# New durations, margins and preferences in the plan of an attention and two-layer MoE kernel, with some low halves on other engines

## The chip, the cores and the metric

The kernel runs on one core of one Trainium2 chip. The metric is the device time of one launch in microseconds (us); several launches are timed and their median is given. One more launch was recorded by the hardware profiler, and all rows below are from that one. The engines are PE (TensorE), ACT (ScalarE), DVE (VectorE), POOL (GpSimd) and SP (SyncE, which here only starts DMA transfers); each works through its own instructions in order.

## The reference

```python
# q, k, v: (4, 8, 576, 64) float32
scores = (1.0 / np.sqrt(64)) * np.matmul(q, k.transpose(0, 1, 3, 2))
kth = np.partition(scores, -32, axis=-1)[..., -32:-31]
scores = np.where(scores >= kth, scores, -1000000000.0)
attn = np.exp(scores - np.max(scores, axis=-1, keepdims=True))
attn = attn / (np.sum(attn, axis=-1, keepdims=True) + 1e-09)
x = np.matmul(attn, v).transpose(0, 2, 1, 3).reshape(2304, 512)
h = x @ moe_w_in                 # 512 x 2048
x = np.maximum(0.01 * h, h) @ moe_w_out   # 2048 x 512
h = x @ moe2_w_in
out = (h * (1.0 / (1.0 + np.exp(-h)))) @ moe2_w_out
```

Each row of 576 scores keeps its 32 largest. The 2304 tokens then go through two layers of the same sizes, the first with a leaky relu, the second with silu.

## The kernel before

**Precision.** Every operand of a matmul is split into a high and a low f16 half, after a scaling by a power of two; a product is then three matmuls (high by high, high by low, low by high). A split is a pass that writes the high half and a pass that writes the low half as the rest. The scale of a tensor comes from its sum of squares, by `pow2` (three small integer operations, L341 to L343).

**Tiling.** The tokens are 18 blocks of 128. A block has 4 pairs of heads, so there are 72 pairs in all. For a pair, PE makes the scores S (L739), ACT copies them to the tile sb (L751), and DVE finds the 32 largest per row by a **chain** of 14 steps, 7 per head: MAX8 finds eight values (L765, L769) and MATCH_REPLACE8 takes them out (L767). ACT then cuts and exponentiates (L791, L800) with a bias of POOL (L779); ACT writes the high half (L815) and POOL the low half (L823) of the result ph; a DMA transpose gives pT, and PE multiplies it by v (pv, L853). ACT, DVE and POOL combine two pairs into half of xf (L887, comb_b, comb_c, with the norm of L868 and L874).

**The layers.** `split_ops` makes the transposed input of a layer: xT for layer 0 from xf, yT for layer 1 from the result acc of layer 0 in PSUM. For yT in the kernel before: square on ACT (L913), scale on POOL, high half on ACT from acc (L934), low half on DVE from acc (L942), DMA transpose (L951). `h_ops` makes a quarter of the hidden layer, 12 matmuls of 128x512 into h (L975), its nonlinearity (ACT L986 in layer 0; ACT L988 and DVE L993 in layer 1), its halves (ACT L1002, POOL L1009) and a DMA transpose to gT (L1014). `o_ops` adds 12 matmuls of a quarter into acc (L1028). These groups of 12 are called **quanta** below: a block and layer have 4 of h and 4 of o, written h0, o0 for layer 0 and h1, o1 for layer 1. acc has one PSUM buffer, shared by both layers and by the sums of weights; h has two, S and pv one each.

**The weights.** `w_ops` brings in the four weight matrices w0 to w3 in 8 pieces each: load, a middle part on ACT (L458), a sign part on DVE (L446), joined on DVE (L467). Of w3 the last pieces come in quarters through one buffer `of`. PE squares the joined pieces (gram, L484), DVE takes the trace (L494), PE sums it over partitions (L542), DVE makes the scale ws (L341 to L343), and then the pieces are scaled and split (ACT L512, DVE L519, or ACT L514 and POOL L524). `w_consts` on POOL (L557 to L561) multiplies the four scales; u2 (POOL L959) needs it, and the nonlinearity of h1 needs u2. In program order the last of the four traces, of w3, so stands ahead of the first quantum of layer 1.

**The order.** Nothing of the order is written out by hand. Every operation is added to a `Plan` with the engine that does it, a duration, what it reads and writes, and a name. `run` is a list scheduler: on each engine, of the operations that may start within `SLACK` of the earliest, it takes the one with the longest remaining chain (`bl`, with durations of some names multiplied by `PACE`) plus a bonus by name (`BOOST`). An operation's earliest time is what its inputs give, plus a margin by name (`LATE`). Layer 0 may be at most `AHEAD` = 2 blocks in front of layer 1. The engines then issue in the order that came out, and on the chip wait for semaphores; the planned times are not used for anything else.

```python
lst.append((max(clock[e], t + LATE.get(o.name, 0.0)), o, max(clock[e], t)))
...
x = min((x for x in lst if x[0] <= t0 + SLACK[e]),
        key=lambda x: (-x[1].bl - BOOST.get(x[1].name, 0), x[1].n))
```

Of the kernel before, what the change touches and what calls it, by code (L numbers as in the profile page):

```python
# [15 lines left out]
ALU = mybir.AluOpType  # L16
# [18 lines left out]
W_MID = ("ACT", "ACT", "ACT", "ACT")  # L35
W_SIGN = ("DVE", "DVE", "DVE", "DVE")
W_LO = (("DVE", "ACT"),) * 4
KV_FUSE = (True, False)
X_FUSE = (True, True)
# [3 lines left out]
PACE = {"h0": 2.45, "h1": 2.45, "o0": 2.45, "o1": 2.45, "chain": 1.1,  # L43
        "wjoin0": 3.0, "wjoin1": 3.0, "wjoin2": 3.0, "wjoin3": 3.0, "wlo0": 2.0, "wlo1": 2.0, "wlo2": 2.0, "wlo3": 2.0}
W_BOOST = 50
LATE = {
    "kvload": 2.0, "qload": 2.0, "store": 1.0, "kvsq": 1.5, "kvsc": 1.0, "kvhi": 1.0, "qsq": 1.5, "qsc": 1.0, "qhi": 1.0,
    "pv": 2.5, "o0": 1.5, "o1": 1.5, "h0": 1.0, "h1": 1.0, "sum": 0.5, "S": 0.3, "cut": 0.3, "g2": 0.3, "comb_b": 0.8,
    "ylo": 0.5, "xlo": 0.5, "norm": 0.5, "gtr": 0.5, "ptr": 0.5, "xtr": 0.5, "ytr": 0.5,
    "kvlo": 0.5, "qlo": 0.5, "qscale": 0.5, "factor": 0.5, "qtr": 0.5, "ktr": 0.5,  # L50
}
BOOST = {
    "g2": 200, "comb_a": 200, "comb_b": 200, "norm": 200, "ylo": 200, "xlo": 200, "kvscale": 200, "wtrace": 200, "wscale": 200,
    "g0": 100, "g1": 100, "ghi": 100, "of": 200, "yhi": 200, "ysq": 200, "s_copy": 100, "cut": 50, "exp": 50, "p_hi": 50,
    "S": 200, "pv": 100, "sum": 200,
}
# [208 lines left out]
def topk_attention_moe_moe2_kernel(  # L265
# [35 lines left out]
    WP = 1024  # L301
# [3 lines left out]
    w_scale = {}  # L305
# [30 lines left out]
    SMALL = {"DVE": 0.1, "POOL": 0.27}  # L336
# [8 lines left out]
    def act_t(n, ptr=0):  # L345
        return 0.13 + 0.00083 * n + 0.09 * ptr
# [38 lines left out]
    def w_ops(i):  # L385
        def mode(c):
            return W_LO[i][c % len(W_LO[i])] if isinstance(W_LO[i], tuple) else W_LO[i]

        for c in range(NWP):
# [3 lines left out]
            for o, n in units:  # L393
# [29 lines left out]
                for o2 in range(0, n, m):  # L423
# [12 lines left out]
                    def sign(o2=o2, m=m, tk=tk, t_of=t_of, raw=raw):  # L436
# [4 lines left out]
                        if W_SIGN[i] == "POOL":  # L441
                            nc.gpsimd.tensor_scalar(
# [675 lines left out]
```

## Time and profile before

| what | value |
|---|---|
| median of 3 launches | 1147.05 us (1145.18 to 1148.27) |
| the profiled launch | 1143.96 us |
| its span, first to last instruction | 1142.2 us |
| PE busy | 986.2 us (86%) |
| DVE busy | 931.5 us (82%) |
| ACT busy | 839.9 us (74%) |
| POOL busy | 622.6 us (55%) |

A row of the timeline gives the start, the duration, the engine, the line of the program, the operation, what it writes and reads with shapes, how many instructions it stands for, and in brackets the idle time of the engine ahead of it with what ended it. An instruction that is pipelined begins before its predecessor's time is over, so the cost of one in a row of equal ones is read from start to start. The page's groups give busy time in all and the mean in ns. The page has no stretch in which all engines are equally loaded: its line of busy tenths has PE at 1 to 4 in the first fifth of the span and at 9 from there on, and DVE at 8 and 9 until near the end, where it falls to 0.

### The profile page before, as it was taken

The numbers are of one execution on the slowest core, as the hardware profiler recorded it, in microseconds if no ns is written. First come the engines' busy times: TensorE is split into PE (matmuls) and PEld (weight loads), VectorE is DVE, ScalarE is ACT, GpSimd is POOL, SyncE is SP. The second block draws the span as 40 slices with busy tenths as digits, with TensorE's granted clock in tenths as the row PEclk, the third lists the DMA queues.
The fourth block names the chain that finished last, engine by engine and source line by source line (L and its number), as shares of the span: only waits on it lengthen the run. The fifth ranks groups of instructions, "written<-read, shape, count | busy, mean of one in ns | idle before, by whom it ended". The sixth has DMA issues, their size and how long they took to land.

```text
span 1142.2 us, 18088 instructions
## 1 busy us (share of the span) xinstructions
PE 986.2 (86%) x6024; PEld 497.1 (44%) x6024; DVE 931.5 (82%) x1906; ACT 839.9 (74%) x1408; POOL 622.6 (55%) x864
## 2 busy tenths in 40 slices
PE   2442248399999899999999999999999999999988
PEld 1222223154445454445455444445454444444443
DVE  5899899999967999999999999984999999810000
ACT  6899879889867877878998778874777777732222
POOL 1545345687655656665757575654666555532221
PEclk9999558699999899999999999999999999999999
DMA  7987865455766866776988767686667666663232
GB/s 208 294 292 218 271 199 111 105 78 109 145 141 124 150 117 125 125 134 137 163 160 141 131 112 146 115 158 129 102 118 131 121 111 123 121 102 65 56 74 56
DMA packets 458110, 157.44 MB, mean 138 GB/s; under 512 B 440864, under 2 KB 449056, under 8 KB 455968
## 3 DMA queue, kind: packets, MB, share of 16 engines
q1 hardware_dynamic: 458016, 156.29, 66.4%
q8 instruction: 47, 0.77, 0.3%
q14 instruction: 47, 0.39, 0.1%
HBM read 47.71 MB, written 4.72 MB: 46 GB/s over the span
## 4 chain that ended last, share of the span: by engine, by line
PE 68%; ACT 8%; DVE 7%; DMA 6%; issue 5%; POOL 3%; SPq 1%; POOLq 0%; ACTq 0%; DVEq 0%
PE h L975 28%; PE acc L1028 28%; PE pv L853 7%; PE S L739 5%; DVE w L767 2%; DVE m L769 1%; DVE w_all L467 1%; DMA w_all<-in_moe_w_in_dram 1%; ACT w_all L418 1%; ACT sb L800 1%; ACT w_all L458 1%; DMA raw<-in_k_dram 1%; DMA w_all<-in_moe_w_out_dram 1%; POOL ph L823 1%; DMA gT<-hl 1%
## 5 line engine op out<-in xcount | busy, mean ns | idle before, releaser
L1028 PE MATMUL acc<-w_all,gT 128*128 128x512 f16 x1728 | 398.4, 381 | 7.6 <-ACT of L1041 3.1
L769 DVE MAX8 m<-w 128x8 f32<-128x576 f32 x432 | 309.6, 746 | 0.0
L1009 POOL TENSOR_TENSOR hl<-g,hl 128x512 f16<-128x512 f32 x144 | 170.3, 1184 | 162.2 <-ACT hl L1002 138.5
L1028 PEld LDWEIGHTS <-gT 128*128 128x128 f16 x1728 | 166.0, 99 | 203.3 <-issue 11.8
L823 POOL TENSOR_TENSOR ph<-sb,ph 128x1152 f16<-128x1152 f32 x72 | 171.2, 2378 | 138.4 <-ACT ph L815 129.7
L767 DVE MATCH_REPLACE8 w<-m,w 128x576 f32<-128x576 f32 x288 | 211.9, 741 | 0.0
L975 PE MATMUL h<-w_all,xT 128*128 128x512 f16 x864 | 200.6, 385 | 2.1 <-DMA xT<-hlx 1.8
L975 PE MATMUL h<-w_all,yT 128*128 128x512 f16 x864 | 196.8, 379 | 0.1
L739 PE MATMUL S<-k,qT 128*128 128x64 f16 (+3 forms) x640 | 94.7, 309 | 57.6 <-ACT sb L751 51.4
L975 PEld LDWEIGHTS <-xT 128*128 128x128 f16 x864 | 85.0, 99 | 104.1 <-issue 7.1
L800 ACT ACTIVATE sb<-sb,nb,u 128x576 f32<-128x576 f32 x144 | 123.4, 858 | 7.1 <-POOL nb L779 4.5
L975 PEld LDWEIGHTS <-yT 128*128 128x128 f16 x864 | 83.9, 98 | 99.1 <-issue 0.4
L791 ACT ACTIVATE sb<-sb,m 128x576 f32<-128x576 f32 x144 | 106.5, 766 | 21.5 <-DVE m L769 21.2
L993 DVE SCALAR_TENSOR_TENSOR g<-g,h 128x512 f32<-128x512 f32 x72 | 49.0, 680 | 87.2 <-ACT g L988 86.7
L853 PE MATMUL pv<-v,pT 128*128 128x128 f16 (+3 forms) x1600 | 110.6, 212 | 9.3 <-DMA pT<-ph 9.3
L751 ACT ACTIVATE sb<-S 128x1152 f32<-128x1152 f32 x72 | 81.1, 1126 | 44.2 <-POOL ph L823 42.2
L853 PEld LDWEIGHTS <-pT 128*128 128x128 f16 (+3 forms) x1600 | 85.9, 101 | 46.3 <-DMA pT<-ph 11.5
L767 DVE MATCH_REPLACE8 w<-m,sb 128x576 f32<-128x576 f32 x144 | 105.8, 741 | 0.0
L765 DVE MAX8 m<-sb 128x8 f32<-128x576 f32 x144 | 102.4, 744 | 3.6 <-ACT sb L751 3.6
L988 ACT ACTIVATE g<-h,u 128x512 f32<-128x512 f32 x72 | 49.3, 684 | 73.4 <-PE h L975 63.7
L779 POOL TENSOR_SCALAR nb<-m,u 128x1 f32<-128x1 f32 x144 | 67.7, 473 | 62.2 <-DVE m L769 50.1
L1002 ACT ACTIVATE hl<-g 128x512 f16<-128x512 f32 x144 | 89.3, 621 | 6.1 <-DVE g L993 3.6
(94 smaller groups left out, 1081.4 us busy)
## 6 DMA issues: line engine op xcount, KB each, us to landing
w_all<-in_moe_w_in_dram SPq DMA_DIRECT2D x16, 1024.0 KB, 7.0
w_all<-in_moe_w_out_dram SPq DMA_DIRECT2D x14, 1024.0 KB, 5.7
raw<-in_k_dram SPq DMA_DIRECT2D x16, 256.0 KB, 3.2
rawq<-in_q_dram SPq DMA_DIRECT2D x32, 128.0 KB, 2.9
raw<-in_v_dram SPq DMA_DIRECT2D x16, 256.0 KB, 3.0
out_dram<-of SPq DMA_DIRECT2D x16, 256.0 KB, 2.6
gT<-hl SPq DMA_TRANSPOSE x144, 3.2
of<-in_moe_w_out_dram SPq DMA_DIRECT2D x8, 256.0 KB, 2.7
```

The lines of the kernel that those rows point to most:

```text
L739: nc.tensor.matmul(out=t[p0:p1, o:o + k1 - k0], lhsT=lhs, rhs=kt[:, k0:k1], start=(x == 0), stop=(x == 1),)
L765: nc.vector.max(m[:, 0], T[sbk][:, h])
L767: nc.vector.match_replace(w, m[:, step // 2], T[sbk][:, h] if step == 1 else w, NEG)
L769: nc.vector.max(m[:, step // 2], w)
L791: nc.scalar.activation(out=x, in_=x, func=AF.Prelu, scale=-1.0, bias=T["m", s][:, h, 3, 7:8], alpha=2.0**-CUT)
L800: nc.scalar.activation(out=x, in_=x, func=AF.Exp, scale=T["u", blk, hf][:, 1, p % 2:p % 2 + 1], bias=T["nb", s][:, h:h + 1], accum_out=T[" ...
L823: nc.gpsimd.tensor_tensor(out=T[phk][:, 1, x0 * S:x1 * S], in0=T[sbk][:, x0:x1].rearrange("p h k -> p (h k)"), in1=T[phk][:, 0, x0 * S:x1 ...
L853: nc.tensor.matmul(out=o[p0:p1, h, p % 2, 0:n], lhsT=l, rhs=r, start=(i == 0), stop=(i == len(mm) - 1))
L975: nc.tensor.matmul(out=t, lhsT=a[:, ai], rhs=w_rhs(layer, wi, kk, i), start=(n == 0), stop=(n == 3 * KDM - 1))
L1002: nc.scalar.activation(out=n[:, 0], in_=T[gk], func=AF.Copy)
L1009: nc.gpsimd.tensor_tensor(out=n[:, 1], in0=T[gk], in1=n[:, 0], op=ALU.subtract)
L1028: nc.tensor.matmul(out=t, lhsT=g[:, ai], rhs=w_rhs2(layer, wi, 4 * i + j), start=(i == 0 and j == 0 and n == 0), stop=(i == NCH - 1 and j ...
```

## The change

The durations in nearly all `add` calls are replaced by others; the margins of `LATE` are all multiplied by 0.55; `PACE` of the quanta goes from 2.45 to 2.85; `BOOST` is a longer table, with names of their own (with a "!") for the operations of block 0. Which engine does what changes in two places: `W_LO` now says it for each piece (one low half of w0 goes from DVE to POOL, with its scaling on ACT; of w2 two scalings go from ACT to POOL, now as a tensor_tensor), and `X_FUSE` of layer 1 is False, so that `split_ops` takes its other branch: ACT scales acc into a tile g (new, L942 of the changed program), ACT makes the high half from g (L949), and POOL the low half (L961) in place of DVE. The instructions of PE are the same in number and shape.

```diff
-W_LO = (("DVE", "ACT"),) * 4
+W_LO = (
+    ("DVE", "ACT", "ACT", "ACT", "DVE", "ACT", "DVE", "ACT"),
+    ("DVE", "ACT"),
+    ("DVE", "ACT", "DVE", "POOL", "DVE", "ACT", "DVE", "POOL"),
+    ("DVE", "ACT", "DVE", "ACT", "DVE", "ACT", "DVE", "ACT"),
+)
...
-X_FUSE = (True, True)
+X_FUSE = (True, False)
...
-    "pv": 2.5, "o0": 1.5, "o1": 1.5, "h0": 1.0, "h1": 1.0, "sum": 0.5, "S": 0.3, "cut": 0.3, "g2": 0.3, "comb_b": 0.8,
+    "qhi": 0.55, "pv": 1.375, "o0": 0.825, "o1": 0.825, "h0": 0.55, "h1": 0.55, "sum": 0.275, "S": 0.165,
...
-    "g2": 200, "comb_a": 200, "comb_b": 200, "norm": 200, "ylo": 200, "xlo": 200, "kvscale": 200, "wtrace": 200, "wscale": 200,
+    "exp": 50, "p_hi": 70, "S": 110, "pv": 100, "sum": 200, "wz2": 0, "wz3": 100, "wmid2": 0, "wmid3": 100,
...
     def act_t(n, ptr=0):
-        return 0.13 + 0.00083 * n + 0.09 * ptr
+        return 0.08 + 0.00085 * n + 0.07 * ptr
...
-                nc.gpsimd.tensor_scalar(y, y, w_scale[i][:, 0:1], None, op0=ALU.mult)
+                nc.gpsimd.tensor_tensor(out=y, in0=y, in1=w_scale[i][:, 0:1].to_broadcast([128, WP]), op=ALU.mult)
...
-        add("PE", 1.02 * len(bs), scores, r=[("qT", blk, hf)] + [("k", b, p) for b in bs], w=[Sk], new=[("S", Sk)],
-            name="S", seq="S")
+        add("PE", 0.84 + 0.15 * len(bs), scores, r=[("qT", blk, hf)] + [("k", b, p) for b in bs], w=[Sk], new=[("S", Sk)],
+            name="S" + tail, seq="S")
...
-            add("DVE", 0.75 if step % 2 else 0.68, chain, r=r, w=[(wk, h), ("m", s, h)],
+            add("DVE", 0.72 if step % 2 else 0.68, chain, r=r, w=[(wk, h), ("m", s, h)],
```

Where the instructions stand moves nearly everywhere. Four places follow, first as before, then as now. Numbers in names only tell buffers apart.

**DVE, from the last join of w3 (w_all from g) to the trace of w3 (junk, wtot).** The steps on m8 and w are the chain of the pairs, den and rec the norm. Before:

```order
L467 SCALAR_TENSOR_TENSOR w_all_70<-w_all_70,g_1699 128x256
L765 MAX m8_1709<-sb_1668 128x8
L767 MATCH_REPLACE w_1710<-m8_1709,sb_1668 128x576 x2
L769 MAX m8_1709<-w_1710 128x8
...
L769 MAX m8_1709<-w_1710 128x8
L767 MATCH_REPLACE w_1710<-m8_1709,w_1710 128x576 x2
L769 MAX m8_1709<-w_1710 128x8
L494 SCALAR_TENSOR_TENSOR junk_69,wtot_1847<-acc_1746,ident_68 128x128
```

Now:

```order
L479 SCALAR_TENSOR_TENSOR w_all_70<-w_all_70,g_1936 128x256
L782 MAX m8_1785<-w_1786 128x8
L778 MAX m8_1960<-sb_1913 128x8 x2
L780 MATCH_REPLACE w_1961<-m8_1960,sb_1913 128x576 x2
L782 MAX m8_1960<-w_1961 128x8
...
L782 MAX m8_1960<-w_1961 128x8
L780 MATCH_REPLACE w_1961<-m8_1960,w_1961 128x576 x2
L782 MAX m8_1960<-w_1961 128x8 x2
L780 MATCH_REPLACE w_1961<-m8_1960,w_1961 128x576 x2
L506 SCALAR_TENSOR_TENSOR junk_69,wtot_2126<-acc_2030,ident_68 128x128
```

Between the last join and the trace stand 8 steps of the chain before and 12 now; from the start of the program to the trace, 149 before and 180 now.

**PE, from the sum of that trace (ones) to the first quantum of layer 1 (yT).** Before (xT and gT quanta are of layer 0):

```order
L542 MATMUL h_1855<-wtot_1847,ones_67 128x1
...
L975 MATMUL h_1886<-w_all_70,xT_1688 128x512
...
L975 MATMUL h_1913<-w_all_70,xT_1688 128x512
...
L1028 MATMUL acc_1968<-w_all_70,gT_1871 128x512
...
L975 MATMUL h_1989<-w_all_70,xT_1688 128x512
...
L1028 MATMUL acc_1968<-w_all_70,gT_1931 128x512
...
L975 MATMUL h_2034<-w_all_70,yT_1613 128x512
```

Now:

```order
L1043 MATMUL acc_1755<-w_all_70,gT_1840 128x512
...
L866 MATMUL pv_1987<-v_326,pT_1915 128x128
...
L496 MATMUL acc_2030<-w_all_70 128x128
...
L752 MATMUL S_2117<-k_305,qT_1901 128x512
...
L554 MATMUL h_2129<-wtot_2126,ones_67 128x1
L554 MATMUL h_2131<-kvssv_2115,ones_67 128x1
...
L990 MATMUL h_2166<-w_all_70,yT_1520 128x512
```

Behind the sum stood five quanta, a block of S and one of pv before the first quantum of layer 1; now that quantum follows at once. Ahead of it on PE stood 14 quanta, 13 blocks of S and 10 of pv; now 16, 15 and 11.

**PE, in the middle, a quantum h of layer 0 (xT) and the quantum o that reads its gT.** Before, h_6364 and gT_6618 belong together:

```order
L975 MATMUL h_6364<-w_all_70,xT_6266 128x512
...
L975 MATMUL h_6399<-w_all_70,xT_6266 128x512
...
L975 MATMUL h_6460<-w_all_70,xT_6266 128x512
...
L975 MATMUL h_6512<-w_all_70,xT_6266 128x512
...
L1028 MATMUL acc_6534<-w_all_70,gT_6277 128x512
...
L1028 MATMUL acc_6775<-w_all_70,gT_6618 128x512
```

Now, h_6511 and gT_6555 belong together:

```order
L990 MATMUL h_6511<-w_all_70,xT_6094 128x512
...
L1043 MATMUL acc_6538<-w_all_70,gT_6433 128x512
...
L866 MATMUL pv_6450<-v_6040,pT_6491 128x128
...
L990 MATMUL h_6588<-w_all_70,xT_6094 128x512
...
L752 MATMUL S_6617<-k_5884,qT_6204 128x512
...
L1043 MATMUL acc_6538<-w_all_70,gT_6555 128x512
```

Between this h and its o stood nine quanta, three pv and three S; now, here, two quanta, a pv and an S.

**PE, near the end, about the last two blocks.** Before, acc_11709 is o0 of block 17, acc_11816 is o1 of block 16, yT_11808 the input of layer 1 of block 17:

```order
L1028 MATMUL acc_11709<-w_all_70,gT_11727 128x512
...
L1028 MATMUL acc_11816<-w_all_70,gT_11760 128x512
...
L1028 MATMUL acc_11816<-w_all_70,gT_11779 128x512
...
L975 MATMUL h_11845<-w_all_70,yT_11808 128x512
```

Now (acc_11701, acc_11849 and yT_11845 are the same three):

```order
L1043 MATMUL acc_11701<-w_all_70,gT_11730 128x512
...
L990 MATMUL h_11815<-w_all_70,yT_11556 128x512
...
L1043 MATMUL acc_11849<-w_all_70,gT_11763 128x512
...
L1043 MATMUL acc_11849<-w_all_70,gT_11796 128x512
...
L1043 MATMUL acc_11849<-w_all_70,gT_11831 128x512
...
L990 MATMUL h_11895<-w_all_70,yT_11845 128x512
```

A quantum of h1 of block 16 (yT_11556) now stands between the last o0 and the first o1, and three o1 instead of two ahead of the first h1 of block 17. After these rows the program goes on with the rest of h1 and o1 of blocks 16 and 17: before, its last quantum of h1 has three o1 of block 17 behind it and one ahead; now all four are behind it.

## Rows read from the trace of the kernel before

**Rows 1.** Busy time of each engine by stretch (columns in its first line)

```profile
core 0: us, PE busy (x) PEld busy (x) DVE busy (x) ACT busy (x) POOL busy (x), PEclk, DMA share, GB/s
28.00:200.00 172.00, 75.69 (x481) 46.12 (x482) 161.68 (x286) 155.62 (x210) 79.98 (x82) 0.82 0.78 230
200.00:255.50 55.50, 35.53 (x249) 20.11 (x249) 55.16 (x110) 46.60 (x79) 39.78 (x49) 0.78 0.49 94
255.50:1100.00 844.50, 834.37 (x5110) 411.50 (x5109) 696.78 (x1471) 611.27 (x1081) 491.38 (x709) 1.00 0.67 123
1100.00:1142.20 42.20, 34.13 (x157) 15.05 (x155) 3.51 (x5) 9.05 (x15) 8.14 (x11) 1.00 0.30 63
```

**Rows 2.** Timeline of DVE about the trace of w3: start, us, instruction

```profile
239.47 0.27 DVE L494 SCALAR_TENSOR_TENSOR junk<-acc,ident 128x128 bf16<-128x128 f32 x1
...
239.66 0.76 DVE L769 MAX8 m<-w 128x8 f32<-128x576 f32 x1
240.34 0.07 DVE L767 MATCH_VALUE_LOAD w<-m,w 128x8 f32 x1
...
241.06 0.08 DVE L767 MATCH_VALUE_LOAD w<-m,w 128x8 f32 x1
...
244.08 1.31 DVE L519 SCALAR_TENSOR_TENSOR w_all<-w_all,ws 128x1024 f16<-128x1024 f32 x1
```

**Rows 3.** Timeline of POOL, w_consts, u2 and a bias

```profile
244.15 1.38 POOL L557 TENSOR_SCALAR wc<-ws,ws,ws 128x1 f32<-128x1 f32 x1
...
246.06 0.65 POOL L959 TENSOR_SCALAR u<-xs,ys,wc 128x1 f32<-128x1 f32 x2
246.69 0.37 POOL L779 TENSOR_SCALAR nb<-m,u 128x1 f32<-128x1 f32 x1
```

**Rows 4.** Timeline of PE about the first quantum of layer 1

```profile
246.26 1.32 PE L853 MATMUL pv<-v,pT 128*128 128x128 f16 x20
...
255.55 2.75 PE L975 MATMUL h<-w_all,yT 128*128 128x512 f16 x12
258.14 1.14 PE L739 MATMUL S<-k,qT 128*128 128x512 f16 x8
```

**Rows 5.** Timeline of PE near the end

```profile
1105.59 5.34 PE L1028 MATMUL acc<-w_all,gT 128*128 128x512 f16 x24 [2.87 <-DVE hlx L942]
...
1126.30 2.75 PE L975 MATMUL h<-w_all,yT 128*128 128x512 f16 x12
...
1135.65 2.76 PE L1028 MATMUL acc<-w_all,gT 128*128 128x512 f16 x12 [1.42 <-DMA gT<-hl]
```

**Rows 6.** Timeline of all engines, the halves of the last yT

```profile
1104.06 0.69 ACT L934 ACTIVATE hlx<-acc,ys 128x512 f16<-128x512 f32 x1
...
1104.78 0.75 DVE L942 SCALAR_TENSOR_TENSOR hlx<-acc,ys,hlx 128x512 f16<-128x512 f32 x1 [8.33 <-ACT hlx L934]
```

**Rows 7.** The page's costliest groups: busy in all, mean ns, idle before

```profile
L1009 POOL TENSOR_TENSOR hl<-g,hl 128x512 f16<-128x512 f32 x144 | 170.3, 1184 | 162.2 <-ACT hl L1002 138.5
L823 POOL TENSOR_TENSOR ph<-sb,ph 128x1152 f16<-128x1152 f32 x72 | 171.2, 2378 | 138.4 <-ACT ph L815 129.7
```

**Rows 8.** Timeline of all engines, two joins of one shape

```profile
201.43 2.37 POOL L823 TENSOR_TENSOR ph<-sb,ph 128x1152 f16<-128x1152 f32 x1 [3.90 <-ACT ph L815]
...
201.87 2.21 DVE L467 SCALAR_TENSOR_TENSOR w_all<-w_all,g 128x256 int32<-128x256 int32 x1
203.76 2.32 POOL L524 TENSOR_TENSOR w_all<-w_all 128x1024 f16<-128x1024 f32 x1
...
208.11 0.40 DVE L467 SCALAR_TENSOR_TENSOR w_all<-w_all,g 128x256 int32<-128x256 int32 x1
```

**Rows 9.** Joins of whole pieces, the line's view: ns min/median/max, first and last start

```profile
L467 DVE SCALAR_TENSOR_TENSOR w_all<-w_all x24: 1196/1220/3147, 23.5 to 137.3; 128x1024 int32<-128x1024 int32 x24
```

**Rows 10.** The same joins, groups of all lines: busy, mean ns, idle before

```profile
L467 DVE SCALAR_TENSOR_TENSOR w_all<-w_all 128x1024 int32<-128x1024 int32 x24 | 33.7, 1409 | 4.6 <-ACT w_all L458 4.6
```

**Rows 11.** Timeline of DVE, signs of the last quarters of w3

```profile
211.40 0.30 DVE L446 TENSOR_SCALAR g<-of 128x256 uint16<-128x256 uint16 x1
...
230.16 0.30 DVE L446 TENSOR_SCALAR g<-of 128x256 uint16<-128x256 uint16 x1
```

More of the change, by code (lines that the diff above doesn't have):

```diff
@@ L601, in square @@
             )
-        add("ACT", act_t(576) + 0.15, square, r=[rk], w=[("kvss", which, b, p)], name="kvsq" + tail)
+        add("ACT", act_t(576) + 0.1, square, r=[rk], w=[("kvss", which, b, p)], name="kvsq" + tail)
         sum_op(("kvss", which, b, p))
@@ L607, in scales @@
             pow2(nc.vector, T["sum", "kvss", which, b, p], sc, scl[which, b][:, 1, p:p + 1])
-        add("DVE", 0.35, scales, r=[("sum", "kvss", which, b, p)], w=[sn], name="kvscale" + tail)
+        add("DVE", 0.38, scales, r=[("sum", "kvss", which, b, p)], w=[sn], name="kvscale" + tail)
         def dst(x):
@@ L665, in square @@
             )
-        add("ACT", act_t(256) + 0.15, square, r=[rk], w=[("qss", blk, hf)], name="qsq" + tail)
+        add("ACT", act_t(256) + 0.12, square, r=[rk], w=[("qss", blk, hf)], name="qsq" + tail)
         eng = "DVE" if first else "POOL"
@@ L672, in scales @@
             pow2(ENG[eng], T["qss", blk, hf], t[:, 0:1], t[:, 1:2])
-        add(eng, 3 * SMALL[eng], scales, r=[("qss", blk, hf)], w=[sn], name="qscale" + tail)
+        add(eng, 0.86 if eng == "POOL" else 0.35, scales, r=[("qss", blk, hf)], w=[sn], name="qscale" + tail)
         if not fuse:
@@ L782, in bias @@
                 )
-            add("POOL", 0.45, bias, r=[("m", s, h), ("u", blk, hf)], w=[("nb", s, h)], name="bias", seq="bias")
+            add("POOL", 0.38, bias, r=[("m", s, h), ("u", blk, hf)], w=[("nb", s, h)], name="bias" + tail, seq="bias")
             def cut(h=h):
@@ L793, in cut @@
                 )
-            add("ACT", act_t(576, 1), cut, r=[("m", s, h)], w=[(sbk, h)], name="cut")
+            add("ACT", act_t(576, 1), cut, r=[("m", s, h)], w=[(sbk, h)], name="cut" + tail)
             def exps(h=h):
@@ L826, in p_lo @@
                 )
-            add("POOL", 0.1 + 0.00205 * n, p_lo, r=[(sbk, h) for h in hs] + [(phk, 0, x0)], w=[(phk, 1, x0)], name="p_lo")
+            add("POOL", 0.06 + 0.002 * n, p_lo, r=[(sbk, h) for h in hs] + [(phk, 0, x0)], w=[(phk, 1, x0)], name="p_lo" + tail)
         def p_transpose():
@@ L899, in comb_c @@
             nc.gpsimd.tensor_tensor(out=dst, in0=dst, in1=r, op=ALU.mult)
-        add("POOL", 0.65, comb_c, r=[("rec", blk, hf)], w=[(xk, hf)], name="comb_c")
+        add("POOL", 0.65, comb_c, r=[("rec", blk, hf)], w=[(xk, hf)], name="comb_c" + tail)
     def split_ops(layer, blk):
         z = "xy"[layer]
+        tail = "!" if blk == 0 and not layer else ""
         src = ("xf", blk) if layer == 0 else ("acc", 0, blk)
@@ L919, in scales @@
             pow2(nc.gpsimd, T["ss", z, blk], t[:, 0:1], t[:, 1:2], 10)
-        add("POOL", 0.75, scales, r=[("ss", z, blk)], w=[sn], name=z + "scale")
+        add("POOL", 0.87, scales, r=[("ss", z, blk)], w=[sn], name=z + "scale" + tail)
         yk = ("f" + z, blk)
```

115 lines of the change are left out of this document (61 added, 54 removed).

## The prediction

> **What bounds the kernel now.** I read the busy times by stretch first [rows 1], and only then single rows, since the bound changes on the way. From 28 to 255.5 us DVE is the bound: it is busy 161.7 of 172.0 us and then 55.2 of 55.5, while PE has work for 111 of these 227.5 us. From 255.5 to 1100 us PE is: 834.4 of 844.5 us, so the whole middle has only 10.1 us in which a better order could gain, and every microsecond that PE waits there is lost. From 1100 us on PE works alone against chains of other engines and waits twice, 2.87 and 1.42 us [rows 5].
>
> The seam is where layer 1 may begin. Its first quantum starts at 255.55 [rows 4]; from there 1142.2 − 255.55 = 886.6 us of span are left, nearly all PE work. So the time is: when layer 1 can begin, plus the PE work not yet done then, plus PE's waits after it. The change leaves PE's work as it is; it can only move these three.
>
> **The change part by part.**
>
> *DVE ahead of the trace of w3.* Before, 149 steps of the chain stand ahead of it, now 180. MAX8 takes 0.68 us from start to start (239.66 to 240.34) and a replacement 0.72 (240.34 to 241.06) [rows 2], so 31 steps at 0.70 are +21.7 us. One low half of w0 leaves DVE: −1.3, the duration of the one at 244.08 [rows 2]; one low half of y: −0.75 [rows 6]. Small operations of scales and norms that cross the trace I put at +0.4, an estimate from their durations of 0.1 to 0.4 us. Sum +20.0: the trace, at 239.47 before [rows 2], comes at 259.5. This takes DVE as packed as it was; its 10.3 us of idle time from 28 to 200 us [rows 1] are the bound below.
>
> *From the trace to layer 1.* After the trace come 0.2 us of its own, one chain step (0.68) and the sum with its scale, then on POOL a bias (0.37), the product of the scales (1.91, from 244.15 to 246.06) and u2 (0.65) [rows 3], and hand-overs between engines, which I take as 0.7 us in all. 259.5 + 0.2 + 0.7 + 0.4 + 1.9 + 0.6 + 0.7 = 264.0. Strictly u2 is wanted by the nonlinearity and not by the quantum, so PE could start two quanta before it (two buffers of h); it would then stand still for the third, which comes to the same. Before, u2 was done at 246.7 [rows 3] and PE reached its first quantum of layer 1 only nine microseconds later, because it had other work first: **the wait for w3 did not cost anything, and now it does.** Layer 1 begins 264.0 − 255.55 = **+8.4 us** later.
>
> *What PE has done by then.* 16 quanta instead of 14, 15 blocks of S instead of 13, 11 of pv instead of 10. A quantum is 2.59 us (255.55 to 258.14), an S 1.14 less the same 0.16 that runs into the next, 0.98, a pv 1.32 [rows 4]: 5.2 + 2.0 + 1.3 = **−8.5 us** from the remaining work. These rows of more work cost nothing ahead of the seam, as PE has 116 us idle there [rows 1]. So the opening is only exchanged: DVE does 20 us more of attention ahead of layer 1, and PE has that much less to do behind it.
>
> *Margins in the middle.* This is the term with no row of its own. With half the margins the plan puts consumers closer to producers: counting PE's rows at 2.59, 0.98 and 1.32 us, half of the o quanta behind the seam had 28 us or more of other PE work between their h and themselves, and 3 of 138 had less than 10 us; now half have 14 us or less, and 16 of 136 less than 10, three of these in the tail. What the chain from h to gT needs is seen where nothing is in its way: the last h1 ends at 1126.30 + 2.75 = 1129.05, its gT is read at 1135.65 [rows 5], 6.6 us. With one low half of ph ahead of it on POOL (2.38) [rows 7] that is 9.0. Of the 13 short distances outside the tail six lie below 9.0: 8.5, 7.5 four times, and 7.8, short by 0.5 + 4 × 1.5 + 1.2 = 7.7 us. POOL is busy some 58% there [rows 1], so I take half, **+4 us**. Bounds: nothing, even −7 if most of the 10.1 us of old waits go; and for the upper end a chain of 11 us, under which 32 distances lie, short by 38 us in all, of which half would be +19.
>
> *The split of y.* ACT has one pass more (0.69), POOL a low half (1.18 by the like one of hl) for DVE's 0.75 [rows 6, 7]. On the chain to yT this is about +1.1 us; it is hidden by the five or more quanta that stand between o0 of a block and h1 of it, and would cost 18 × 1.1 = 20 us if none did. In sum ACT has 18 × 0.6 = 11 us more, POOL 18 × 1.18 = 21 us; in the middle they are busy 72% and 58% [rows 1], so neither becomes the bound. acc in PSUM is free sooner, after the scaling pass rather than after DVE's.
>
> *The tail.* The wait of 2.87 us is of o1 of block 16 for acc, which ylo of block 17 still reads [rows 5, 6]; now a quantum (2.59) stands between, and the pass that frees acc ends about as early as ACT's did, at 1104.75, 2.1 us after the square began. The wait of 1.42 is for the last gT; now three quanta, 7.8 us, stand between its h and its o, against the 6.6 us of the chain. And the first h1 of block 17 has four quanta, 10.4 us, ahead of it for a chain of 8 to 9.5 us. So **−4.3 us**.
>
> *Other moves.* One low half of w0 and two scalings of w2 go to POOL, which is busy 120 of 227.5 us ahead of the seam [rows 1]; no consumer waits for them before layer 0 or layer 1 needs the piece, which I cost at nothing, or at 2.3 us if a join stood behind one. By the rows, DVE pays for a busy POOL: a join of 128x256 took 2.21 us beside a low half of ph on POOL (201.43 to 203.80), and 0.40 alone [rows 8]. The 24 joins of whole pieces take 1.41 us in the mean and 1.22 in the median [rows 9, 10], 4.4 us lost; the 64 other joins and signs, read in the same two views, lose another 14.6, so some 19 us in all.
> The Trainium skill (SBUF — State Buffer, Who interferes with whom) says that DVE and GpSimd share one pair of ports, and that an operation of either with the pair blocks the other for its whole length; a DVE operation with two inputs in SBUF contends with any GpSimd operation that reads SBUF. The trace agrees, 2.21 us against 0.40. By that rule the 9 us of work that POOL gets ahead of the seam (three passes over a piece of weights at 2.3, two low halves of y at 1.18) would raise the 19 us by 9/120, an estimate of 1.4 us more on DVE, and the sum would be 1148.1.
>
> **Sum.** 8.4 − 8.5 + 4 − 4.3 = −0.4 us. The profiled execution is 1143.96 us around a span of 1142.2; it would be 1143.6. The median stands 3.1 us above the profiled one, so the forecast is **1146.7 us**, no change that can be measured. About 0.3%, or 3.4 us, is what can be told from no change: faster is below 1143.6, slower above 1150.5.
>
> **The rivals.**
>
> *Forecast: the opening is exchanged one for one.* Its own range is 1142 to 1152: the middle term from 0 to +8, the seam ±3, in which I count that PE's granted clock, 0.78 from 200 to 255.5 us and 1.00 behind [rows 1], may stay low for a quantum or two after PE has waited there.
>
> *Rival 1, slower: PE waits for gT in the middle.* Place: the o quanta from 350 to 1010 us that now follow their h by 7.5 to 11 us. For it: PE has no slack there at all, and ACT and POOL get more to do. Against it: the longest distances are cut most and those of pv to its S stay above 25 us. Price: +19 instead of +4, 1161.7. It decides from +7.8 on, when the middle's idle time goes from 10 to 18 us.
>
> *Rival 2, faster: DVE gets through the opening in less time.* For it: DVE has 10.3 us of idle time and some 19 us of stalls ahead of the seam that another order need not have, and an order made with the right durations is made to fit them. If half of the idle time and a third of the stalls go, 5 + 6 = 11 us, the trace comes at 248 and the seam is again where PE's queue puts it, at about 253: 1146.7 − 11 = 1135.7. Against it: the idle time lies between 28 and 200 us, where DMA and the first weights set the pace.
>
> *Rival 3, slower: the quarters of w3 become the bound.* The last signs lie 211.40 to 230.16, 18.76 us for three steps, 6.25 each [rows 11], through one buffer; by the steps of DVE that now stand between them they would have 5.5 us. If the loads cannot follow, DVE waits 0.7 us for each of eight: +5.6, 1152.3. Against it: these signs showed almost no wait for a load before, 0.1 us for all eight, so the load was not what set 6.25.
>
> **How the numbers follow.** Forecast 0.41, rival 1 0.20, rival 2 0.27, rival 3 0.12. Rival 2 lies faster for nearly all, the forecast for a quarter of it: 0.25 + 0.12 = 0.37. Slower are nearly all of rival 1, two thirds of rival 3 and a quarter of the forecast: 0.19 + 0.05 + 0.09 = 0.33; same is the rest, 0.30. The range reaches from below rival 2 to rival 1: 1133 to 1163.
>
> **What would show it.** The trace of w3 on DVE at about 259, the first yT quantum at about 264 with PE idle a few microseconds ahead of it; idle time of PE from there to the tail some 14 us, with gT the releaser; no waits of PE at acc or the last gT in the tail. A trace at or below 250 is rival 2; PE idle time above 20 us in the middle is rival 1; DVE idle ahead of the signs by the quarter loads is rival 3. The sum is wrong if a low half of y on POOL makes h1 wait in the middle, which I cost at nothing.

## The result

The changed kernel takes **1127.82 us** (median of 4 runs, 1126.64 to 1128.32) against 1146.12 before (4 runs, 1143.29 to 1148.27): ratio 0.984, 95% interval 0.9816 to 0.9865. It is 18.3 us faster; no change that can be measured was forecast. The profiled execution is 1127.61 us with a span of 1125.8, 16.4 below that of before. Times below are medians of runs at the usual clock; two runs at a lower one, 1184.45 us with the new margins alone and 1163.15 us with the factor 0.998, are left out.

The page of the changed kernel, first the instructions and the busy time of each engine over the whole span, then the busy tenths in 40 slices of the two engines that take turns as the bound:

```profile
span 1125.8 us, 18127 instructions
...
PE 983.3 (87%) x6024; PEld 493.7 (44%) x6024; DVE 917.2 (81%) x1887; ACT 858.4 (76%) x1425; POOL 654.7 (58%) x885
...
PE   1533384479999999999999999999999999999998
DVE  5999999997966999999999999984999999720000
```

By stretch, the rows that answer to [rows 1] (columns as there; the last stretch ends with the span):

```profile
28.00:200.00 172.00, 81.77 (x538) 47.96 (x538) 169.66 (x299) 158.70 (x213) 92.31 (x96) 0.68 0.78 227
200.00:255.50 55.50, 37.00 (x242) 20.39 (x243) 53.03 (x104) 47.73 (x85) 38.62 (x44) 0.78 0.61 127
255.50:1100.00 844.50, 836.95 (x5123) 412.02 (x5121) 677.47 (x1444) 628.84 (x1092) 515.85 (x727) 1.00 0.66 123
1100.00:1125.80 25.80, 22.12 (x103) 9.82 (x101) 2.75 (x4) 6.64 (x10) 4.61 (x4) 0.99 0.28 62
```

DVE is busy 169.7 of 172 us instead of 161.7: its idle time from 28 to 200 us went from 10.3 to 2.3 us. PE's waits, from the first quantum of layer 1 to 1100 us, are (who waited at which line, for what, us in all, times, longest):

```profile
PE S L752 <- ACT sb L764: 2.4, 7, 0.8
PE acc L1043 <- ACT of L1056: 1.6, 1, 1.6
PE h L990 <- DMA xT<-hlx: 1.5, 1, 1.5
PE h L990 <- DVE g L1008: 1.3, 2, 0.8
PE h L554 <- ACT junk L610: 0.3, 1, 0.3
```

Behind 1100 us there is none. The kernel before had these behind its first quantum of layer 1 (the second view of waits is that of before, from 255.5 to 1100 us; the two of [rows 5] come on top):

```profile
PE h L542 <- ACT junk L598: 3.2, 2, 2.8
PE acc L1028 <- ACT of L1041: 3.1, 2, 2.4
PE pv L853 <- DMA pT<-ph: 1.5, 2, 0.9
PE S L739 <- ACT sb L751: 1.3, 2, 1.1
PE S L739 <- DMA k<-hlk: 0.5, 1, 0.5
PE h L975 <- DVE fx L341: 0.2, 1, 0.2
```

The seam, PE's timeline of the changed kernel, with DVE's trace of w3 and POOL's u2 (each its own view). They answer to [rows 2 to 4]:

```profile
249.76 6.17 PE L496 MATMUL acc<-w_all 128*128 128x128 bf16 x64 [4.36 <-ACT g L942]
...
256.75 0.28 PE L554 MATMUL h<-wtot,ones 128*128 128x1 f32 x2
...
257.27 2.75 PE L990 MATMUL h<-w_all,yT 128*128 128x512 f16 x12
259.86 1.32 PE L866 MATMUL pv<-v,pT 128*128 128x128 f16 x20
...
264.38 2.75 PE L990 MATMUL h<-w_all,yT 128*128 128x512 f16 x12 [0.49 <-DVE g L1008]
267.95 5.40 PE L990 MATMUL h<-w_all,yT 128*128 128x512 f16 x24 [0.83 <-DVE g L1008]
```

```profile
256.04 0.29 DVE L506 SCALAR_TENSOR_TENSOR junk<-acc,ident 128x128 bf16<-128x128 f32 x1 [2.49 <-PE acc L496]
```

```profile
257.50 0.34 POOL L569 TENSOR_SCALAR wc<-ws,ws,ws 128x1 f32<-128x1 f32 x1
...
258.35 0.66 POOL L974 TENSOR_SCALAR u<-xs,ys,wc 128x1 f32<-128x1 f32 x2
```

So the last link to the trace was not DVE. The gram of w3 on PE (L496) and the result of a block of layer 0 share the one buffer acc; the gram had to wait until ACT had scaled that result into g (L942, done at 249.71), with PE idle for 4.36 us, and DVE then waited 2.49 us for the gram.

**Where the 16.4 us of span went.** Layer 1 starts at 257.27 instead of 255.55: +1.7. PE has 8.5 us less work left there (two quanta, two S and a pv more are done, as the prediction counted). PE waits 7.1 instead of 14.1 us behind it: −7.0, of which −4.3 in the tail. That leaves −2.6, and nearly all of it is the clock. In the kernel before PE waited three times within some 8 us, and then ran at the lower of its two levels (the granted clock was 0.63 from 392 to 400 us, against 1.00 in the same stretch now):

```profile
385.85 2.73 PE L853 MATMUL pv<-v,pT 128*64 128x128 f16 x40 [0.90 <-DMA pT<-ph]
391.40 0.58 PE L542 MATMUL h<-kvssv,ones 128*128 128x1 f32 x2 [2.82 <-ACT junk L598]
393.10 2.08 PE L739 MATMUL S<-k,qT 128*128 128x512 f16 x8 [1.11 <-ACT sb L751]
394.97 4.24 PE L1028 MATMUL acc<-w_all,gT 128*128 128x512 f16 x12
```

An S took 2.08 instead of 1.14 us and a quantum 4.24 instead of 2.75, which is 2.4 us of the 2.6. Sum: 1.7 − 8.5 − 7.0 − 2.6 = −16.4.

### The profile page after: what moved, and what is told of

Read it like the earlier page. It is cut to its first block, busy times and chain, and to the rows that moved or that the text cites. A ratio compares the mean times of both kernels' runs of the same rounds, so it can differ in the third digit from the quotient of the medians.

```text
span 1125.8 us, 18127 instructions
## 1 busy us (share of the span) xinstructions
PE 983.3 (87%) x6024; PEld 493.7 (44%) x6024; DVE 917.2 (81%) x1887; ACT 858.4 (76%) x1425; POOL 654.7 (58%) x885
## 4 chain that ended last, share of the span: by engine, by line
PE 46%; DVE 24%; ACT 11%; POOL 7%; issue 6%; DMA 5%; SPq 1%; ACTq 0%; POOLq 0%; DVEq 0%
PE acc L1043 20%; PE h L990 18%; DVE w L780 7%; DVE m L782 6%; PE pv L866 4%; DVE w_all L479 3%; PE S L752 3%; POOL ph L836 2%; DMA pT<-ph 2%; DVE m L778 2%; ACT sb L813 2%; POOL hl L1024 2%; DVE w_all L458 2%; ACT ph L828 1%; ACT sb L804 1%
## 5 line engine op out<-in xcount | busy, mean ns | idle before, releaser
L1043 PEld LDWEIGHTS <-gT 128*128 128x128 f16 x1728 | 166.1, 98 | 205.7 <-issue 10.6
L804 ACT ACTIVATE sb<-sb,m 128x576 f32<-128x576 f32 x144 | 108.8, 765 | 23.3 <-DVE m L782 22.9
L752 PE MATMUL S<-k,qT 128*128 128x64 f16 (+3 forms) x640 | 91.0, 302 | 30.1 <-DMA qT<-hlx 12.0
L828 ACT ACTIVATE ph<-sb 128x1152 f16<-128x1152 f32 x72 | 83.5, 1160 | 4.9 <-DMA pT<-ph 3.5
## 6 DMA issues: line engine op xcount, KB each, us to landing
raw<-in_k_dram SPq DMA_DIRECT2D x16, 256.0 KB, 3.3
raw<-in_v_dram SPq DMA_DIRECT2D x16, 256.0 KB, 3.0
out_dram<-of SPq DMA_DIRECT2D x16, 256.0 KB, 2.4
of<-in_moe_w_out_dram SPq DMA_DIRECT2D x8, 256.0 KB, 2.9
```

The costliest lines, as they stand in the source:

```text
L752: nc.tensor.matmul(out=t[p0:p1, o:o + k1 - k0], lhsT=lhs, rhs=kt[:, k0:k1], start=(x == 0), stop=(x == 1),)
L804: nc.scalar.activation(out=x, in_=x, func=AF.Prelu, scale=-1.0, bias=T["m", s][:, h, 3, 7:8], alpha=2.0**-CUT)
L828: nc.scalar.activation(out=T[phk][:, 0, x0 * S:x1 * S], in_=T[sbk][:, x0:x1].rearrange("p h k -> p (h k)"), func=AF.Copy)
L1043: nc.tensor.matmul(out=t, lhsT=g[:, ai], rhs=w_rhs2(layer, wi, 4 * i + j), start=(i == 0 and j == 0 and n == 0), stop=(i == NCH - 1 and j ...
```

## The experiments

**Four kernels in the order of the changed one, with one delay each.** Each repeats an instruction on the same inputs, so the computed values stay.

Trace of w3 on DVE 31 times:

```diff
-            nc.vector.scalar_tensor_tensor(
+            for _ in range(31 if i == 3 else 1):
+                nc.vector.scalar_tensor_tensor(
```

> The changed program in its order, with the trace of w3 on DVE done 31 times instead of once: 30 more passes of 0.22 us (start to start 256.04 to 256.26), 6.6 us more on DVE directly ahead of the sum that PE needs before layer 1. Theory: the start of layer 1 is set by DVE and nothing behind it gives time back, so the time rises by all of it, 1127.8 + 6.6 = 1134.4 us. Rival: PE or u2 have slack there, under +2, below 1130 us.

Measured 1138.37 us, +10.6. A pass took 0.33 us, not 0.22, as reading the accumulator follows each; 30 of them are 9.9 us. PE's timeline:

```profile
266.28 0.59 PE L555 MATMUL h<-wtot,ones 128*128 128x1 f32 x2 [9.49 <-DVE junk L507]
...
267.16 5.07 PE L991 MATMUL h<-w_all,yT 128*128 128x512 f16 x12
273.32 10.53 PE L991 MATMUL h<-w_all,yT 128*128 128x512 f16 x48
```

Layer 1 starts 9.9 us later, and the span behind that start is 869.2 instead of 868.5 us. The theory holds in so far: what delays the trace delays layer 1, and it comes back nowhere. PE's waits for u2 (1.3 us) are gone, but the first quantum behind the wait takes 5.07 us, 2.3 more than elsewhere, and the next four 2.6 each. What sets the trace itself is not shown by this run: here too it waits 2.56 us for the gram.

First product of `w_consts` on POOL 15 times:

```diff
-        nc.gpsimd.tensor_scalar(
+        for _ in range(15):
+            nc.gpsimd.tensor_scalar(
```

> The changed program in its order, with the first product of w_consts on POOL done 15 times: 14 more at 0.43 us (257.50 to 257.93), so u2 about 6.0 us later, at 265, near where the prediction put it (264.0). The prediction's step, that a late u2 costs as much as a late first quantum of layer 1: +6, 1133.8 us. Rival: PE has two quanta of h, for which there are buffers, and a pv to do ahead of the first that waits for u2, so only what is beyond them is lost: about +2.5, 1130.3 us.

Measured 1132.55, +4.7. POOL and PE:

```profile
256.30 7.42 POOL L570 TENSOR_SCALAR wc<-ws,ws,ws 128x1 f32<-128x1 f32 x15
...
264.22 0.66 POOL L975 TENSOR_SCALAR u<-xs,ys,wc 128x1 f32<-128x1 f32 x2
```

```profile
256.07 2.75 PE L991 MATMUL h<-w_all,yT 128*128 128x512 f16 x12
...
266.06 4.44 PE L991 MATMUL h<-w_all,yT 128*128 128x512 f16 x12 [3.38 <-DVE g L1009]
```

A repetition took 0.49 us in the mean, not 0.43. u2 is done 8.8 us behind the first quantum instead of 1.7, so 7.1 later; PE loses 2.7 us of waiting more (4.0 instead of 1.3) and 1.7 by a quantum at the lower clock. Nearly two thirds of the lateness are paid: less than the prediction's step says, and more than the rival, which had the waiting right and left out the clock.

Low half of g on POOL three times, in the five tightest quanta of layer 0:

```diff
-            nc.gpsimd.tensor_tensor(out=n[:, 1], in0=T[gk], in1=n[:, 0], op=ALU.subtract)
+            for _ in range(3 if (layer, blk, i) in ((0, 5, 0), (0, 8, 1), (0, 8, 2), (0, 9, 3), (0, 15, 2)) else 1):
+                nc.gpsimd.tensor_tensor(out=n[:, 1], in0=T[gk], in1=n[:, 0], op=ALU.subtract)
```

> The changed program in its order, with the low half of g on POOL done three times instead of once in the five quanta of layer 0 whose o stands within 7.8 us behind their h: 2.3 us more in each chain. Theory: such a chain ends about 1.3 us before its o (in the profile of the changed kernel the transpose issued at 614.90 lands some 3.2 us later and the o starts at 619.40), so PE waits 1.0 us five times: +5, 1132.8 us, up to 1135 if the granted clock falls after a wait. Rival: there is more slack than that, no more than +1, 1128.8 us.

Measured 1135.74, +7.9. PE now waits for gT three times (1.28, 1.57, 1.11 us), where it did not at all, and once for S behind a delayed POOL; there the clock falls too:

```profile
457.15 2.76 PE L1044 MATMUL acc<-w_all,gT 128*128 128x512 f16 x12 [1.28 <-DMA gT<-hl]
...
621.30 2.08 PE L752 MATMUL S<-k,qT 128*128 128x512 f16 x8 [2.41 <-ACT sb L764]
```

So the short distances that were delayed had about 1 us of slack (2.3 us of delay, waits of 1.1 to 1.6), as the theory said; the cost came out above its range by the wait for S and by the clock.

Sum of squares on ACT five times, for three pairs of k:

```diff
-            nc.scalar.activation(
+            for _ in range(5 if (which, b, p) in (("k", 2, 0), ("k", 2, 1), ("k", 3, 1)) else 1):
+                nc.scalar.activation(
```

> The changed program in its order, with the sum of squares on ACT done five times instead of once for three pairs of k (2.7 us more of ACT each) ahead of sums that stand in PE's queue. Theory: where PE waits some 3 us in the middle the clock falls for a few us as well, as in the kernel before at 391 us (a wait of 2.8 and 1.1 us, then S in 2.08 instead of 1.14 us and a quantum in 4.24 instead of 2.75), so each place costs up to 5 us, 15 in all: 1143 us. Rival 1: the wait costs itself alone: 2.5 us each, 1135 us. Rival 2: the sums have slack, no PE wait: within 2 us of 1127.8.

Measured 1136.37, +8.5: PE waits 5.8 us more in the middle, nearest to rival 1. After a wait of 2.77 us the work runs at the full clock (granted clock 1.00 from 424 to 436 us); after one of 2.50 a pv and a quantum take 1.71 and 3.94 us, 1.6 more than elsewhere (0.76 from 646 to 652 us):

```profile
429.20 1.14 PE L753 MATMUL S<-k,qT 128*128 128x512 f16 x8 [2.77 <-ACT sb L765]
```

```profile
648.27 0.38 PE L554 MATMUL h<-kvssk,ones 128*128 128x1 f32 x2 [2.50 <-ACT junk L611]
648.51 1.71 PE L867 MATMUL pv<-v,pT 128*128 128x128 f16 x20
650.16 3.94 PE L991 MATMUL h<-w_all,yT 128*128 128x512 f16 x12
```

**Seven plans made anew with a part of the change undone, or alone.** The program is built by the plan, so each has an order of its own.

The split of y as before in the changed kernel:

```diff
-X_FUSE = (True, False)
+X_FUSE = (True, True)
```

> The changed program with the split of y as before (X_FUSE True for layer 1: low half on DVE from PSUM), planned anew. In its order PE has 857.3 us of work left at the first quantum of layer 1 (860.9 in the changed program), 196 chain steps ahead of the trace of w3 (180), and near the end a quantum of h1 stands between the last o0 and the first o1 as in the changed program, but only three o1 behind the last h1 as before. Theory: the gain is the order's (margins, preferences, durations) and the split of y itself is worth little: the last wait of 1.4 us comes back, seam about the same, 1127 to 1132 us. Rival: the split of y carries the gain in the middle (acc free sooner): above 1137 us.

1151.56 us. The theory misses, and the rival, above 1137, has the side right but not the reason: the trace of w3 comes at 267.2 us and layer 1 at 269.3 (16 more chain steps stand ahead), and PE waits 16.7 us behind it, only 0.3 us of it for acc as in the kernel before. Ahead of the seam the gram of w3 waits 3.2 us for that low half of y, and the trace 0.7 us for the gram.

The new `BOOST` and `PACE` alone in the kernel before, the new durations alone, the new margins alone (tables swapped whole):

> The kernel before with only the new BOOST and PACE tables (no new durations, margins or engines). In its order 859.6 us of PE work are left at the first quantum of layer 1 (869.4 before, 860.9 changed), 184 chain steps ahead of the trace (149 before), and the end of the program is as before. Theory: it gets the exchange in the opening (+1.7 us of start, -9 of work, some waits), and neither the tail nor the middle: about 1146 - 6 = 1140 us. Rival 1: it gets all, the tables are the change: under 1132 us. Rival 2: the prediction's zero-sum exchange: 1144 to 1148 us.

> The kernel before with only the measured durations in the plan. In its order 872.0 us of PE work are left at the first quantum of layer 1 (869.4 before), 152 chain steps ahead of the trace, end of the program as before except that o1 follows o0 at once. Theory: durations alone move PE's waits in the middle (those of 2.8 and 2.4 us, with the clock that falls behind them, may go: up to -6), but leave the opening and the tail: 1140 to 1147 us. Rival: the durations are what the gain comes from: under 1133 us.

> The kernel before with only the halved margins. In its order 872.0 us of PE work are left at the first quantum of layer 1 (869.4 before), 149 chain steps ahead of the trace; half of the o quanta stand 23 us or more behind their h (28 before, 14 in the changed program), 2 under 10 us. The prediction's step (halved margins make PE wait more in the middle): 1147 to 1152 us. Rival: margins were waste and their halving saves waits in the opening: 1138 to 1143 us.

1155.99, 1163.65 and 1156.84 us: **every part that was tried alone makes the kernel before slower**, by some 10 to 17 us. No theory comes near; for the margins alone the direction was right. The first does the exchange in the opening (layer 1 begins 11.9 us later, with 9.8 us less PE work left) and loses another 10 us behind it. The split of y and `W_LO` were not tried alone.

The old durations, the old `BOOST`, the old `W_LO` in the changed kernel:

> The changed program with the durations of the kernel before in the plan. In its order 868.4 us of PE work are left at the first quantum of layer 1 (860.9), 164 chain steps ahead of the trace (180), the end as in the changed program, half of the o quanta within 13.6 us of their h. Theory: measured durations are what lets the tight order run without waits; with the old ones PE waits some 20 us behind the start of layer 1 instead of 7: 1138 to 1150 us. Rival: durations matter little once tables and the split of y are new: 1126 to 1133 us.

> The changed program with the preferences (BOOST) of the kernel before. In its order 863.2 us of PE work are left at the first quantum of layer 1 (860.9), 168 chain steps ahead of the trace (180), the end as in the changed program; low halves of ph are no longer put behind those of g on POOL. Theory: without that preference PE waits for gT where o stands 7.5 us behind its h (12 such quanta below 8 us): 1133 to 1142 us. Rival: preferences matter little: 1126 to 1131 us.

> The changed program with the low halves of the weights on the engines of the kernel before (W_LO). 859.6 us of PE work left at the first quantum of layer 1 (860.9), 180 chain steps ahead of the trace as in the changed program, distances of o behind h the same (half within 14.0 us). Theory (the table of low halves has no part in the gain but through the plan): if this neighbour keeps the changed program's order in the middle, 1126 to 1131 us; if not, 1135 to 1150 us. Rival (two scalings and a low half on POOL unload ACT and DVE ahead of layer 1): the first quantum of layer 1 comes 2 to 3 us later, 1130 us.

1147.66, 1141.14 and 1139.60 us. The old durations lose all of the gain. The old `BOOST` keeps the few waits (7.6 us behind the seam) and loses by a layer 1 that begins at 266.1; its time is in the range of its theory, but by luck, since PE's waits for gT come to 0.8 us. The old `W_LO` has as many chain steps ahead of the trace, but the trace at 264.7 and layer 1 at 266.9, since DVE there is busy 5.8 us more (228.5 instead of 222.7) and idle 2.8 us more (1.1 us of it for the gram, which waits 2.3 us for acc). Its expectation, no part in the gain but through the middle, and its rival, 2 to 3 us, both miss the place or the size. No run has the old margins in the changed kernel.

**Plans next door.** Since no part carried the gain, the question was whether the changed plan is a lucky one. All planned durations were multiplied by one factor, in either kernel:

```diff
+        dur = dur * 0.998
         o = Op()
```

> The changed program with every planned duration multiplied by 0.998, a change without meaning, planned anew. In its order 859.6 us of PE work are left at the first quantum of layer 1 (860.9 in the changed program), 182 chain steps ahead of the trace (180), the end of the program the same. Theory now held: how much PE waits behind the start of layer 1 is an accident of the single plan, so this plan comes out some us off the changed one, 1130 to 1140 us. Rival: the new durations, margins and preferences give good plans as a class, so a neighbour is as good: 1125 to 1130 us.

> The changed program with every planned duration multiplied by 1.01, planned anew. In its order 861.9 us of PE work are left at the first quantum of layer 1 (860.9), 168 chain steps ahead of the trace (180): 12 fewer, so layer 1 may begin 8 us earlier with 1 us more of work. Theory now held (the outcome is that of the single plan): 1125 to 1140 us, not to be told ahead. Rival (neighbours are as good): within 1122 to 1130 us.

> The kernel before with every planned duration multiplied by 1.002. In its order 872.0 us of PE work are left at the first quantum of layer 1 (869.4 before), 149 chain steps ahead of the trace, the end different in a few quanta. Theory A (each single plan is a draw with a spread of tens of us, of which both timed kernels are good ones): slower than before, 1150 to 1170 us. Theory B (only the changed program's plan is touchy): within 4 us of 1146.5.

> The kernel before with every planned duration multiplied by 0.99. In its order 873.6 us of PE work are left at the first quantum of layer 1, 154 chain steps ahead of the trace (149). Theory A (every plan is a draw): 1150 to 1175 us. Theory B (only the changed program's plan is touchy): within 4 us of 1146.5.

> The changed program with every planned duration multiplied by 1.002. PE work left at the first quantum of layer 1 (860.9 us) and chain steps ahead of the trace (180) are those of the changed program, so its opening should be too. If the opening is what the plan has to get right, 1126 to 1132 us; if the waits in the middle are an accident of each plan, 1135 to 1150 us.

> The changed program with every planned duration multiplied by 0.99, the partner of the kernel before at 0.99 (1165.0 us). 861.9 us of PE work left at the first quantum of layer 1 (860.9), 173 chain steps ahead of the trace (180), end of the program the same. Theory (the changed plans are better as a class by some 20 us on top of a spread of each plan): 1130 to 1150 us. Rival (a good draw and no class): 1150 to 1165 us, no better than its partner by more than 5 us.

> The kernel before with every planned duration multiplied by 1.01, the partner of the changed program at 1.01 (1161.8 us). PE work left (869.4 us), chain steps ahead of the trace (149) and the end of the program are those of the kernel before. Theory (the changed plans are better as a class): above 1165 us if the class holds here too. Rival (a plan with the same opening has the same time): within 4 us of 1146.5, faster than its partner by 15 us.

| factor | kernel before, us | changed, us | difference |
|---|---|---|---|
| 0.99 | 1164.96 | 1137.54 | −27.4 |
| 0.998 | not run | 1144.42 | |
| 1.000 | 1146.12 | 1127.82 | −18.3 |
| 1.002 | 1151.02 | 1128.26 | −22.8 |
| 1.01 | 1151.26 | 1161.80 | +10.5 |

A factor of 0.998 costs the changed kernel 16.6 us, one of 1.01 34 us. Before, the same kind of step costs 5 to 19. None of the neighbours that were run is faster than the kernel in their middle. Of four pairs three have the changed side ahead, by 18 to 27 us, and one behind by 10.5; the mean is −14.5, and −13.2 without the pair at 1.000, whose two plans are the fastest of their columns. So there is both: a class that may be better, and a spread from plan to plan as large as the gain. Four pairs with this spread do not settle how much better the class is.

Where a plan loses is seen by splitting its span at the first quantum of layer 1. The work left is counted in the program's order, by the durations that the prediction used for a quantum, an S and a pv; the last column is the rest of the span less that work (waits, slow clock, the end, and what the count is off by). The rows are of the profiled executions; that of before at 1.002 lies 4.5 us above its median, the others within 2.2 us of theirs:

| plan | layer 1 begins, us | span behind it, us | PE work left, us | rest less work, us |
|---|---|---|---|---|
| before | 255.6 | 886.7 | 869.4 | 17 |
| before, 1.002 | 258.1 | 895.7 | 872.0 | 24 |
| before, 0.99 | 259.4 | 904.0 | 873.6 | 30 |
| before, 1.01 | 258.2 | 891.0 | 869.4 | 22 |
| changed | 257.3 | 868.5 | 860.9 | 8 |
| changed, 1.002 | 256.5 | 868.0 | 860.9 | 7 |
| changed, 0.998 | 260.2 | 882.5 | 859.6 | 23 |
| changed, 0.99 | 259.9 | 875.9 | 861.9 | 14 |
| changed, 1.01 | 270.3 | 889.2 | 861.9 | 27 |
| changed, old BOOST | 266.1 | 871.8 | 863.2 | 9 |

At 1.01 12 fewer steps stand ahead of the trace, and layer 1 yet begins 13 us later: DVE is busy 223.4 of 240.1 us up to the trace, so idle 16.6 instead of 5.3 us. At 0.998 the opening is 3 us worse, and most of the rest is in PE's waits, 18.2 instead of 7.1 us. The first rows of its view of waits, behind the start of layer 1:

```profile
PE pv L867 <- DMA pT<-ph: 5.4, 4, 2.5
PE S L753 <- ACT sb L765: 4.2, 4, 1.8
```

They are the kinds of waits that the other plans have too, at other places. One wait is common to a class: that of acc for the low half of y on DVE, 2.9 to 6.9 us in each of the seven profiled plans of the kernel before or with one part of the change. Where the split of y is new it cannot occur, as DVE no longer reads acc for it; the view of waits has PE wait 0.3 us behind the seam for the pass on ACT that frees acc instead in one plan (old durations), and not at all in the others. But the order can avoid most of that wait too: it is 0.3 us with the split of y as before in the changed kernel.

## Why the prediction was wrong

**The frame was right.** The time is the start of layer 1, plus the PE work left there, plus PE's waits behind it, to which the clock behind a wait has to be added; the work term (−8.5 us) and the tail (−4.3) came out as predicted. The last quanta of the changed kernel run without a gap:

```profile
1098.65 2.75 PE L990 MATMUL h<-w_all,yT 128*128 128x512 f16 x12
1101.24 2.75 PE L1043 MATMUL acc<-w_all,gT 128*128 128x512 f16 x12
1103.83 7.93 PE L990 MATMUL h<-w_all,yT 128*128 128x512 f16 x36
1111.60 10.52 PE L1043 MATMUL acc<-w_all,gT 128*128 128x512 f16 x48
```

**The seam: +8.4 was predicted, it is +1.7**, with 1.3 us of PE's waits behind it that belong there, so it is off by 5.4 us. The step that failed is the one that took DVE as packed as it was. The trace of w3 comes at 256.0, not 259.5: DVE's busy time up to it grew by 21.9 us (200.8 to 222.7), near the 20.0 of the sum, but its idle time fell from 10.6 to 5.3 us, half of which is the wait for the gram (2.49). Without that wait DVE would have been at the trace at 253.55. The sum has no term for the gram: in the kernel before it was done at 236.71, 2.8 us ahead of the trace, and now it ends at 255.93, as acc came free late and as its 64 matmuls took 6.17 instead of 4.90 us (granted clock 0.59 over them):

```profile
231.81 4.90 PE L484 MATMUL acc<-w_all 128*128 128x128 bf16 x64
```

The idle time that went is half of rival 2, and it was written down as a rival only because the order was taken to be as packed as before. The other half did not come: measured against the median duration of each shape, the 88 joins and signs lost 19.4 us in all, and by the same count 18.3 before. Of rival 3 there is no sign, as DVE waited 0.4 us for one quarter of w3.

From the trace to u2 it is 3.0 us instead of 4.5; the first product of `w_consts` took 0.34 us, not the 1.38 of [rows 3], which was one instruction of one execution. And the step that a late u2 costs as much as a late quantum is only two thirds right, by the experiment on POOL; in the changed kernel layer 1 began 1.7 us before u2 was done.

**The middle: +4 was predicted, it is −6.6** (waits 9.8 to 5.8 us, and 2.6 of clock), off by 10.6 us and of the wrong sign. Rival 1 did not come, as PE's waits for gT there were zero. Two steps failed. First, the short distances were put down to the margins. The margins alone leave half of the o quanta 23 us or more behind their h, and the other parts alone 26 to 27 us; with one other part undone it is 13 to 14 us all the same. So the distance comes from several parts together; whether the margins are needed for it no run shows. Second, the price of a short distance. It assumed that a low half of ph stands ahead of the low half of g on POOL every second time. In the changed kernel, behind the h of 609.31 to 612.06 and ahead of its o at 619.40, the view of all engines has:

```profile
612.34 0.58 ACT L1001 ACTIVATE g<-h 128x512 f32<-128x512 f32 x1
...
612.95 0.63 ACT L1017 ACTIVATE hl<-g 128x512 f16<-128x512 f32 x1
...
613.71 1.16 POOL L1024 TENSOR_TENSOR hl<-g,hl 128x512 f16<-128x512 f32 x1 [3.92 <-ACT hl L1017]
...
614.83 2.38 POOL L836 TENSOR_TENSOR ph<-sb,ph 128x1152 f16<-128x1152 f32 x1
614.90 1.24 SPq L1029 DMA_TRANSPOSE gT<-hl  x1
```

The low half of g goes first and that of ph follows it at once. The transpose lands some 3.2 us behind its issue, near 618.1, 1.3 us ahead of the o. 2.3 us more in five such chains cost 7.9 us. So **the slack is about 1 us, and it was enough, as in none of the five a low half of ph (2.38 us) stands ahead of that of g.** One may think of the new preferences, which put "p_lo" 90 and "glo" 20 back. But with the old `BOOST` the eight quanta of layer 0 with distances of 7.5 to 7.8 us have no low half of ph between h and the low half of g either, and the view of waits has only:

```profile
PE acc L1042 <- DMA gT<-hl: 0.8, 2, 0.5
```

A reading that fits both, though no run tests it: the scheduler puts an o where its gT is planned to be ready, so short distances stand just where the chain is free, and half of them cannot be charged with what stands elsewhere. What is behind the old waits (the sum for k and v, the store, pv) was not costed at all, beyond a bound of −7, and neither was the clock behind them. That bound held nearly the whole term, and it should have been given a chance of its own. (In the chances, a quarter of the forecast's 0.41 is 0.10 on either side, not 0.12 and 0.09; this changes little.)

**The split of y, the engines and the low halves** were costed at nothing. On the paths that the prediction looked at this was right: PE waits for no yT. On one that it did not look at, the pass that frees acc for the gram, the split of y takes part in the seam. Undone in the plan, the split of y and the low halves cost 24 and 12 us, since all else moves too.

**What stays open.** The gain of 16.4 us is accounted for row by row. Which part of the change it is due to has no answer from these runs: each undone part loses between 12 and 24 us, each part tried alone loses 10 to 17, and 0.2% on all durations may lose 17. That a class of plans is better by some 15 us is what four pairs point to, and not more than that.

## What to carry to other kernels

Where a list scheduler makes the order, a change of its tables is a new draw of the whole order: read the order that came out, and give the bounds at least the spread that neighbouring tables show, before any term is costed. Split the span at the point where the bound changes, and add up when the second engine can start, what it has left, and its waits behind. Follow the start back over every buffer on its way, not only along the busiest engine. Delays put in on purpose (one instruction repeated) tell how much slack each term has. A short distance between producer and consumer isn't a price by itself: look at what else stands between on each engine of the chain.

## What the runs showed of the hardware

The granted clock of PE does not follow a single wait's length. After 9.49 us of waiting one quantum took 5.07 us and the next four 2.6 each; after 3.38 us a quantum took 4.44; after 2.77 us S stayed at 1.14 us; after 2.50 a quantum took 3.94, after 2.41 S took 2.08, and after 0.90, 2.82 and 1.11 us within some 8 us an S and a quantum took 2.08 and 4.24 (at the full clock 1.14 and 2.75). So a single wait of 2.4 to 2.8 us cost itself alone, or itself and some 1.6 us more; the three waits together cost 2.4 us more.
